# Beacon attention followed by a two-layer feed-forward net: the first batch in an order written out by hand

## The chip, the cores and the metric

The kernel runs on one core of a Trainium2 chip. A core has five engines that run side by side, each through its own list of instructions in order: TensorE (matrix products, PE in the profile), VectorE (DVE), ScalarE (ACT), GpSimd (POOL) and SyncE (SP). They wait for one another by semaphores. Data comes from the chip's main memory by DMA; a DMA is issued by one of the engines, and 16 DMA engines carry it out. The metric is the time of the program on the device in microseconds (us), lower being better.

## The reference

There are 8 batches of 8 heads with 576 positions of 64 elements, and each head has 16 beacon positions ahead of its keys and values, which every query may see. The other keys are seen causally. The attention's output is laid out as 4608 tokens of 512 elements and goes through two layers with a leaky rectifier between them.

```python
k_all = np.concatenate([beacon_k, k], axis=2)
v_all = np.concatenate([beacon_v, v], axis=2)
scores = scale * np.matmul(q, k_all.transpose(0, 1, 3, 2))
causal[:, Nb:] = np.triu(np.ones((S, S), dtype=bool), k=1)
scores = np.where(causal, -1000000000.0, scores)
a = np.exp(scores - scores.max(-1, keepdims=True))
a /= a.sum(-1, keepdims=True) + 1e-09
attn_out = np.matmul(a, v_all)
x = attn_out.transpose(0, 2, 1, 3).reshape(B * S, H * D)
h = x @ w_in                      # 512 -> 2048
g = np.maximum(0.01 * h, h)
out = g @ w_out                   # 2048 -> 512
```

## The kernel before

**Units of work.** Heads are handled in pairs; pair g is number hp = g mod 4 of batch b = g div 4, so there are 32 pairs. Two pairs make a group of four heads, and q and k come per group: `load_qk(b, grp)` issues four DMAs (L139) on GpSimd's queue into the raw buffers `q_raw` and `k_raw`, converted to bfloat16 on the way. `permute` (L149) copies a raw buffer into `q_nat` or `k_nat` with the order of its elements changed. `load_v(b)` (L180 to L190) issues six DMAs of fp32 values on SyncE's queue, and `cast_v` (L198) makes five copies to bfloat16, one for each block of keys, into one of two buffers `v_aug` with a column of ones.

**One pair.** `t_q(g, 0)` and `t_q(g, 1)` transpose q and k on TensorE (L217), and VectorE copies the result out (L222). `score(g, n)`, n from 0 to 3, multiplies (L240) into one of two buffers `sc`, and ScalarE takes the exponential (L251, L255) into `aT`. `masks(g)` multiplies the blocks on the diagonal by a triangle of ones and zeros, in three VectorE instructions (L265, L272, L278). `value(g, 0)` and `value(g, 1)` multiply by V (12 and 18 matmuls, L306; the column of ones gives the sums), and VectorE takes the reciprocal (L315) and scales (L316). The second half reads all five blocks of V. `x_transposes(g)` transposes the result (L328) and copies it into `xT` (L333). Buffers limit how far ahead a pair may run: two sets of `qT` and `kT`, three of `aT`, two of `x_nat`, two of each raw buffer, two of `v_raw`.

**The feed-forward part** is cut into nine chunks of 512 tokens. `moe1` is one of 16 steps of the first layer of a chunk (four matmuls, L342, and a rectifier on ScalarE, L349), `moe2` a quarter of one of its four output tiles in the second (L358, copied out at L367). `fill()` writes down the next such step that is ready; `ready[0]` says how many chunks may be begun. Steps for the first chunk can begin once batch 0's `xT` is complete.

**The order.** Nothing is planned by costs: the program writes each engine's list in the order of its own calls (`tc.manual_schedule`), and an engine never takes a later instruction first. At the head stand the loads: q and k of (0, 0), then of (0, 1); beacon keys on ScalarE's queue; V of batch 0 on SyncE's, held until the first load of k has landed; w_in in four parts and q and k of batch 1 on GpSimd's. After a first `beacon_transposes`, `permute` of (0, 0) in halves and the transposes of pair 0, the main loop runs over g. In round g it writes the transposes of pair g + 1, scores of pair g, values of pair g - 1, and `x_transposes` of pair g - 2, and at the end `masks(g)`. For batch 0 there are some special steps in it:

- in round 0, behind the scores, the beacon transposes for all other batches, `cast_v(0)` on VectorE and the permutes of (0, 1) on VectorE, and only then `masks(0)`;
- in round 1, the four loads of w_out on GpSimd's queue;
- in round 2, `load_v(1)`, held until the second exponential of pair 2 is done, and the permutes of (1, 0) on GpSimd; in round 3 those of (1, 1) and `cast_v(1)` on GpSimd;
- in round 4, the last values and transposes of batch 0, then `ready[0] = 1` and three fills ahead of the transposes of pair 4.

The lines of the head and of round 0 that matter:

```python
        load_v(0, after=first[1])
        make_mask()
        make_ones()
        for i in range(4):
            load_w_in(i)
...
            if g == 0:
                beacon_transposes(1, B)
                cast_v(0, nc.vector)
                for which in range(2):
                    permute(0, 1, which, nc.vector.tensor_copy)
...
            if has(g):
                masks(g)
```

Of the kernel before, what the change touches and what calls it, by code (L numbers as in the profile page):

```python
# [15 lines left out]
def kernel(  # L16
# [50 lines left out]

    singles = ctx.enter_context(tc.tile_pool(name="singles", bufs=1))
    rawpool = ctx.enter_context(tc.tile_pool(name="rawpool", bufs=2))
    natpool = ctx.enter_context(tc.tile_pool(name="natpool", bufs=3))  # L70
    headpool = ctx.enter_context(tc.tile_pool(name="headpool", bufs=2))
    gpool = ctx.enter_context(tc.tile_pool(name="gpool", bufs=2))
# [34 lines left out]
            nc.gpsimd.memset(t[:, :, :, D : D + 1], 1.0)  # L107

    def load_w_in(i):
        nc.gpsimd.dma_start(  # L110
            out=w_in_sb[:, :, i * 512 : (i + 1) * 512], in_=w_in_r[:, :, i * 512 : (i + 1) * 512]
        )

# [9 lines left out]
    def load_qk(b, grp):  # L123


        qk_raw[b, grp] = (
            rawpool.tile([128, 2, RI, D], BF16, name="q_raw"),
            rawpool.tile([128, 2, RI, D], BF16, name="k_raw"),
        )
        nat[b, grp] = (  # L130
            natpool.tile([128, RI, 2, D], BF16, name="q_nat"),
            natpool.tile([128, RI, 2, D], BF16, name="k_nat"),
        )
# [12 lines left out]
    def permute(b, grp, which, copy, p0=0, p1=128):  # L146

        src, dst = qk_raw[b, grp][which], nat[b, grp][which]
        copy(out=dst[p0:p1], in_=src[p0:p1].rearrange("p h i d -> p i h d"))  # L149

# [22 lines left out]

    v_raws = {}

    def load_v(b, after=None):

        t = rawpool.tile([128, NKB, H, D], FP32, name="v_raw")
        v_raws[b] = t
        first = nc.sync.dma_start(out=t[0:NB, 0], in_=beacon_v[b].rearrange("h p d -> p h d"))  # L180
        if after is not None:
            tc.add_manual_dep(
                first.ins,
                after.ins.name,
                mybir.DependencyInfo(mybir.DependencyClass.Sync, mybir.DependencyReason.DATA),
                reason="loads in order of need",
            )
        nc.sync.dma_start(out=t[NB:128, 0], in_=v[b, :, 0:112].rearrange("h p d -> p h d"))
        for c in (1, 2, 3, 4):
            nc.sync.dma_start(  # L190
                out=t[0 : ROWS[c], c],
                in_=v[b, :, OFF[c] : OFF[c] + ROWS[c]].rearrange("h p d -> p h d"),
            )

    def cast_v(b, eng):
        t, dst = v_raws.pop(b), v_bufs[b % 2]
# [205 lines left out]
    with order:  # L402
# [1 line left out]
        make_identity(nc, ident)  # L404
        load_qk(0, 1)
        load_beacon_k()
        load_v(0, after=first[1])
        make_mask()
        make_ones()
        for i in range(4):  # L410
            load_w_in(i)
        load_qk(1, 0)
        load_qk(1, 1)
# [4 lines left out]
            permute(0, 0, 1, nc.scalar.copy, e * RP, (e + 1) * RP)  # L418
        t_q(0, 0)
        t_q(0, 1)  # L420

        def loads(g):
            b, hp = divmod(g, NPAIR)
            if 1 <= b < B - 1:
# [7 lines left out]
            if hp == 3 and b < B - 1:  # L432
                cast_v(b + 1, nc.gpsimd)

        for g in range(NG + 2):
            b, hp = divmod(g, NPAIR)
            if has(g):
                loads(g)
            if g == NPAIR:

                value(g - 1, 0)
                x_transposes(g - 2)
                value(g - 1, 1)
                x_transposes(g - 1)
                ready[0] = 1
                for n in range(3):
                    fill()
                t_q(g, 0)
# [16 lines left out]
                if slots[n]:  # L465
                    fill()

            if has(g + 1) and g + 1 != NPAIR:
                t_q(g + 1, 0)
            if has(g):  # L470
                score(g, 0)
                last = score(g, 1)
                if g == 2:
                    load_v(1, after=last)
            slot(0)
            if has(g - 2) and g - 2 != NPAIR - 1:
# [5 lines left out]
            if has(g - 1):  # L482
                value(g - 1, 0)
            slot(2)
            slot(3)
            if has(g + 1) and g + 1 != NPAIR:
# [5 lines left out]
            if has(g - 1):  # L492
                value(g - 1, 1)
            slot(5)
            slot(6)
            if g == 0:
                beacon_transposes(1, B)
                cast_v(0, nc.vector)
                for which in range(2):
                    permute(0, 1, which, nc.vector.tensor_copy)  # L500
            if g == 1:
                for i in range(4):
                    load_w_out(i)
            if has(g):
                masks(g)
            slot(7)
# [32 lines left out]
```

## Time and profile before

| what | value |
|---|---|
| time, median of 3 runs | 390.72 us (389.57 to 391.29) |
| the profiled execution, time | 390.62 us |
| its span | 388.9 us |
| TensorE busy | 352.4 us, 91% of the span |
| VectorE, ScalarE, GpSimd busy | 176.6, 197.9, 99.5 us |
| first matmul of the feed-forward part (L342) | 53.72 us from the start of the span |
| bytes moved by DMA | 33.52 MB |

The page cuts the span into 40 equal slices of 9.7 us. A digit is the busy share of a slice in tenths.

```profile
PE   2306689999999999999999999999999999999996
DVE  3307956965555655465546554655455331101021
ACT  4304439945575556555655566456645623343310
POOL 8306336876204520462046203200000000000000
DMA  8996999777343913482248225100010001101012
```

From the seventh slice on TensorE is full to the last one. In the first six it isn't, and the third slice has no digit above zero on any compute engine, while the row of the DMA engines is full there.

Times in the prediction are microseconds from the start of the span. In a timeline the first two numbers of a row are the start and the length; a row that ends in "x12" merges twelve instructions, and the length is from the first one's start to the last one's end.

### The profile page before, as it was taken

What the parts mean: (1) busy time and instruction counts of PE and PEld (TensorE: products, weight loads), DVE (VectorE), ACT (ScalarE), POOL (GpSimd) and SP (SyncE); (2) the same over time, 40 slices, a digit from 0 to 9 for tenths busy, and PEclk for the clock granted to TensorE, in tenths of its full rate; (3) what the DMA queues carried; (4) which work ended last, traced back from release to release, by engine and by line L of the source; (5) the groups of instructions that cost most, each with busy time, mean ns of one, the idle gap of its engine ahead of it and who ended that gap; (6) DMA issues with size and microseconds to landing.
All of it is one profiled execution on the core that took longest, in us unless ns stands there. A gap on an engine that the chain in (4) does not pass through costs nothing.

```text
span 388.9 us, 7644 instructions
## 1 busy us (share of the span) xinstructions
PE 352.4 (91%) x3240; PEld 183.7 (47%) x3240; DVE 176.6 (45%) x401; ACT 197.9 (51%) x308; POOL 99.5 (26%) x145
## 2 busy tenths in 40 slices
PE   2306689999999999999999999999999999999996
PEld 1104455655555555555555555555555454444442
DVE  3307956965555655465546554655455331101021
ACT  4304439945575556555655566456645623343310
POOL 8306336876204520462046203200000000000000
PEclk9999689999999999999999999999999999999999
DMA  8996999777343913482248225100010001101012
GB/s 132 202 197 90 186 206 199 142 112 123 71 96 58 161 46 82 71 140 66 76 78 128 77 65 91 56 29 27 2 56 29 28 9 47 55 1 54 29 54 81
DMA packets 58354, 33.52 MB, mean 86 GB/s; under 512 B 41424, under 2 KB 53712, under 8 KB 58320
## 3 DMA queue, kind: packets, MB, share of 16 engines
q0 software_dynamic: 13440, 13.64, 23.2%
q1 hardware_dynamic: 43840, 19.14, 20.3%
q8 instruction: 25, 0.41, 0.4%
q10 hardware_dynamic: 1040, 0.26, 0.3%
q14 instruction: 9, 0.07, 0.1%
HBM read 37.22 MB, written 9.44 MB: 120 GB/s over the span
## 4 chain that ended last, share of the span: by engine, by line
PE 88%; DMA 5%; DVE 2%; SPq 2%; ACT 0%; issue 0%; POOL 0%; DVEq 0%; POOLq 0%
PE acc L358 33%; PE acc L342 33%; PE av L306 8%; PE sc L240 7%; PE tp L217 5%; DMA v_raw<-in_v_dram 4%; PE tp L328 2%; SPq L190 2%; DVE aT L265 1%; DMA k_raw<-in_k_dram 1%; DVE aT L272 0%; ACT aT L251 0%; DVE x_nat L316 0%; DVE q_nat L149 0%; POOL q_raw L139 0%
## 5 line engine op out<-in xcount | busy, mean ns | idle before, releaser
L342 PE MATMUL acc<-xT,w_in_sb 128*128 128x512 bf16 x576 | 145.0, 380 | 0.0
L349 ACT ACTIVATE gT<-acc 128x512 bf16<-128x512 f32 x144 | 85.8, 598 | 110.6 <-PE acc L342 110.5
L358 PE MATMUL acc<-w_out_sb,gT 128*128 128x512 bf16 x576 | 142.0, 380 | 0.0
L251 ACT ACTIVATE aT<-sc 128x928 bf16<-128x928 f32 (+2 forms) x128 | 102.7, 857 | 58.4 <-PE sc L240 58.4
L358 PEld LDWEIGHTS <-gT 128*128 128x128 bf16 x576 | 51.2, 98 | 61.5 <-issue 7.5
L342 PEld LDWEIGHTS <-w_in_sb 128*128 128x128 bf16 x576 | 52.5, 98 | 56.0 <-issue 2.9
L367 DVE COPY osb<-acc 128x512 f32<-128x512 f32 x36 | 24.9, 691 | 58.6 <-PE acc L358 57.2
L306 PEld LDWEIGHTS <-aT 128*128 128x128 bf16 (+1 forms) x960 | 39.2, 101 | 20.1 <-DVE aT L265 4.4
L306 PE MATMUL av<-v_aug,aT 128*128 128x65 bf16 (+1 forms) x960 | 42.6, 198 | 5.4 <-DVE aT L265 4.1
L240 PE MATMUL sc<-qT,kT 64*128 64x208 bf16 (+5 forms) x384 | 43.1, 302 | 1.7 <-DVE kT L222 1.0
L222 DVE COPY qT<-tp 128x576 bf16<-128x576 bf16 x32 | 24.1, 753 | 28.2 <-PE tp L217 28.1
L149 POOL COPY q_nat<-q_raw 128x1152 bf16<-128x1152 bf16 x14 | 16.2, 1155 | 78.8 <-PE tp L217 72.4
L315 DVE RECIPROCAL rec<-av 128x6 f32<-128x6 f32 x64 | 12.0, 188 | 53.3 <-PE av L306 53.2
L217 PE MATMUL tp<-ident,q_nat 64*128 64x64 bf16 x288 | 14.7, 197 | 20.1 <-DVE q_nat L149 20.1
L316 DVE TENSOR_TENSOR x_nat<-av,rec 128x384 bf16<-128x384 f32 x64 | 31.4, 491 | 2.2
L222 DVE COPY kT<-tp 128x576 bf16<-128x576 bf16 x32 | 24.2, 756 | 16.6 <-PE tp L217 16.6
L333 DVE COPY xT<-tp 128x576 bf16<-128x576 bf16 x32 | 14.6, 456 | 27.2 <-PE tp L328 27.1
L198 POOL CAST v_aug<-v_raw 128x512 bf16<-128x512 f32 (+1 forms) x35 | 22.5, 682 | 15.0 <-DMA v_raw<-in_v_dram 12.6
L217 PEld LDWEIGHTS <-q_nat 64*128 64x128 bf16 x288 | 10.9, 98 | 32.4 <-DVE q_nat L149 20.7
L139 POOL DMA_DIRECT2D q_raw<-in_q_dram x32 | 20.2, 631 | 20.1 <-DVE q_nat L149 19.1
L149 POOL COPY k_nat<-k_raw 128x1152 bf16<-128x1152 bf16 x14 | 16.2, 1160 | 30.8 <-PE tp L217 30.7
L240 PEld LDWEIGHTS <-kT 64*128 64x128 bf16 (+1 forms) x384 | 19.8, 100 | 5.2 <-issue 3.0
(30 smaller groups left out, 158.0 us busy)
## 6 DMA issues: line engine op xcount, KB each, us to landing
out_dram<-osb SPq DMA_DIRECT2D x36, 256.0 KB, 2.0
v_raw<-in_v_dram SPq DMA_DIRECT2D x24, 256.0 KB, 5.2
q_raw<-in_q_dram POOLq DMA_DIRECT2D x32, 144.0 KB, 5.1
k_raw<-in_k_dram POOLq DMA_DIRECT2D x32, 144.0 KB, 5.6
w_in_sb<-in_moe_w_in_dram POOLq DMA_DIRECT2D x4, 512.0 KB, 13.4
w_out_sb<-in_moe_w_out_dram POOLq DMA_DIRECT2D x4, 512.0 KB, 11.8
v_raw<-in_v_dram SPq DMA_DIRECT2D x8, 224.0 KB, 4.3
v_raw<-in_v_dram SPq DMA_DIRECT2D x8, 160.0 KB, 5.1
```

The costliest lines, as they stand in the source:

```text
L149: copy(out=dst[p0:p1], in_=src[p0:p1].rearrange("p h i d -> p i h d"))
L198: eng.tensor_copy(out=dst[0 : ROWS[c], c, :, 0:D], in_=t[0 : ROWS[c], c])
L217: nc.tensor.transpose(ps[:, i * RP : (i + 1) * RP], nat[b, grp][which][ps_, i].rearrange("p h d -> p (h d)"), ident[ps_, ps_],)
L222: nc.vector.tensor_copy(out=dst.rearrange("c (p i) -> c p i", i=RI), in_=ps[:, 0:S].rearrange("c (i p) -> c p i", i=RI),)
L240: nc.tensor.matmul(out=sc[0 : ROWS[c], par, col - c0 : col - c0 + w], lhsT=kT[ps_, c * 128 : c * 128 + ROWS[c]], rhs=qT[ps_, q0 : q0 + w], ...
L251: last = nc.scalar.activation(out=aT[:, :, c0 : c0 + w], in_=sc[:, :, 0:w], func=AF.Exp, scale=0.125)
L306: nc.tensor.matmul(out=avv[:, n, 0 : D + 1], lhsT=aT[0 : ROWS[c], par, a0 : a0 + 128], rhs=va[0 : ROWS[c], c, 2 * hp + par, :], start=(c = ...
L316: nc.vector.tensor_tensor(out=x_nat[:, t0:t1].rearrange("p t e d -> p (t e) d"), in0=avv[:, :, 0:D], in1=rec[:, n0:n1, None].to_broadcast( ...
L342: nc.tensor.matmul(out=acc, lhsT=w_in_sb[:, j, fc * 128 : (fc + 1) * 128], rhs=xT[:, j, i * 512 : (i + 1) * 512], start=(j == 0), stop=(j ...
L349: nc.scalar.activation(out=gT[i][:, fc, :], in_=acc, func=AF.Prelu, alpha=0.01)
L358: nc.tensor.matmul(out=acc, lhsT=gT[i][:, fc, t * 128 : (t + 1) * 128], rhs=w_out_sb[:, fc, :], start=(fc == 0), stop=(fc == NF - 1),)
L367: nc.vector.tensor_copy(out=osb, in_=acc)
```

## The change

Batch 0 leaves the main loop and is written out call by call; the loop begins at round 4. Scores run up to two pairs ahead of the values. `cast_v(0)` and the permutes of (0, 1) change places with other VectorE work. `load_w_in(0)` is made to wait for the last DMA of V of batch 0 (`behind`), and all later work on GpSimd's queue stands behind it. The raw buffers of q and k go from two to four, and the buffers `q_nat` and `k_nat` are taken when the permute is written, not with the load. The loads of w_out move behind the permutes of batch 1 on GpSimd's queue, two behind each group. `load_v(1)` is still held by the second exponential of pair 2. From round 4 on the loop's calls are the same as before.

```diff
+    qkpool = ctx.enter_context(tc.tile_pool(name="qkpool", bufs=4))
...
         qk_raw[b, grp] = (
-            rawpool.tile([128, 2, RI, D], BF16, name="q_raw"),
-            rawpool.tile([128, 2, RI, D], BF16, name="k_raw"),
-        )
...
+            qkpool.tile([128, 2, RI, D], BF16, name="q_raw"),
+            qkpool.tile([128, 2, RI, D], BF16, name="k_raw"),
         )
...
+    def behind(ins, other):
+        tc.add_manual_dep(
+            ins.ins,
+            other.ins.name,
+            mybir.DependencyInfo(mybir.DependencyClass.Sync, mybir.DependencyReason.DATA),
+            reason="loads in order of need",
+        )
...
-        load_v(0, after=first[1])
+        v0 = load_v(0, after=first[1])
         make_mask()
         make_ones()
-        for i in range(4):
+        behind(load_w_in(0), v0)
+        for i in range(1, 4):
             load_w_in(i)
         load_qk(1, 0)
         load_qk(1, 1)
...
         t_q(0, 0)
         t_q(0, 1)
+        score(0, 0)
+        score(0, 1)
+        t_q(1, 0)
+        t_q(1, 1)
+        score(0, 2)
+        score(0, 3)
+        beacon_transposes(1, B)
+        score(1, 0)
+        score(1, 1)
+        masks(0)
+        permute(0, 1, 0, nc.vector.tensor_copy)
+        permute(0, 1, 1, nc.vector.tensor_copy)
+        t_q(2, 0)
+        t_q(2, 1)
+        score(1, 2)
+        score(1, 3)
+        score(2, 0)
+        v1 = score(2, 1)
+        masks(1)
+        cast_v(0, nc.vector)
+        value(0, 0)
+        for which in range(2):
+            permute(1, 0, which, nc.gpsimd.tensor_copy)
+        load_w_out(0)
+        load_w_out(1)
+        for which in range(2):
+            permute(1, 1, which, nc.gpsimd.tensor_copy)
+        load_w_out(2)
+        load_w_out(3)
+
+        score(2, 2)
+        load_v(1, after=v1)
+        score(2, 3)
+        t_q(3, 0)
+        t_q(3, 1)
+        value(0, 1)
+        score(3, 0)
+        score(3, 1)
+        masks(2)
+        x_transposes(0)
+        value(1, 0)
+        score(3, 2)
+        value(1, 1)
+        score(3, 3)
+        x_transposes(1)
+        value(2, 0)
+        value(2, 1)
+        masks(3)
+        x_transposes(2)
+        value(3, 0)
+        value(3, 1)
+        x_transposes(3)
+        cast_v(1, nc.gpsimd)
+        ready[0] = 1
...
-        for g in range(NG + 2):
+        for g in range(NPAIR, NG + 2):
```

More of the change, by code (lines that the diff above doesn't have):

```diff
@@ L181, in load_v @@
         if after is not None:
[L182 to L187, printed above, removed]
+            behind(first, after)
         nc.sync.dma_start(out=t[NB:128, 0], in_=v[b, :, 0:112].rearrange("h p d -> p h d"))
         for c in (1, 2, 3, 4):
-            nc.sync.dma_start(
+            last = nc.sync.dma_start(
                 out=t[0 : ROWS[c], c],
@@ L481 @@
             slot(1)
-            if has(g - 1):
+            if has(g - 1) and g - 1 >= NPAIR:
                 value(g - 1, 0)
@@ L485 @@
             slot(3)
-            if has(g + 1) and g + 1 != NPAIR:
+            if has(g + 1):
                 t_q(g + 1, 1)
```

36 lines of the change are left out of this document (12 added, 24 removed).

## The prediction, on record before the changed kernel ran

> **What bounds the kernel now.** I read the stages first, cut at three instants: the first cast of V, the end of the casts, and the first matmul of the feed-forward part (columns: length of the stage, then busy microseconds and instructions of each engine, granted clock, DMA share, GB/s).
>
> ```profile
> 0.00:14.83 14.83, 5.62 (x56) 3.51 (x56) 5.73 (x12) 7.99 (x9) 11.62 (x26) 1.00 0.98 158
> 14.83:31.46 16.63, 0.00 (x0) 0.00 (x0) 2.06 (x5) 0.00 (x0) 0.00 (x0) 1.00 1.10 181
> 31.46:53.72 22.26, 15.47 (x213) 11.44 (x213) 18.83 (x40) 10.35 (x15) 10.54 (x14) 0.78 1.02 164
> 53.72:388.90 335.18, 331.30 (x2974) 168.73 (x2972) 149.99 (x345) 179.60 (x284) 77.30 (x106) 1.00 0.35 73
> ```
>
> The last stage is TensorE's: busy for 331.30 of 335.18 us. Nothing in it can be won by an order of work at the start; it can only begin earlier. The second stage is empty: 16.63 us without one matmul, and the DMA engines full. The third has TensorE busy for 15.47 of 22.26 us and VectorE for 18.83. So the change is worth what it takes out of the first 53.72 us, less what it makes late behind them.
>
> Why the second stage is empty is in the waits of that window and the timelines of VectorE and TensorE (start, length, instruction; in brackets the idle time before it and its releaser):
>
> ```profile
> DVE v_aug L198 <- DMA v_raw<-in_v_dram: 14.6, 4, 6.2
> ```
> ```profile
> 14.83 0.43 DVE L198 CAST v_aug<-v_raw 128x512 bf16<-128x512 f32 x1
> ...
> 31.12 0.43 DVE L198 CAST v_aug<-v_raw 80x512 bf16<-80x512 f32 x1 [0.39 <-DMA v_raw<-in_v_dram]
> 31.46 0.74 DVE L149 COPY q_nat<-q_raw 128x1152 bf16<-128x1152 bf16 x1
> ...
> 37.47 3.92 DVE L265 TENSOR_TENSOR aT<-aT,mask 128x224 bf16<-128x224 bf16 x1
> 41.31 1.49 DVE L272 TENSOR_TENSOR aT<-aT,mask 128x768 bf16<-128x768 bf16 x1
> ...
> 49.95 0.27 DVE L265 TENSOR_TENSOR aT<-aT,mask 128x224 bf16<-128x224 bf16 x1
> 50.14 0.55 DVE L272 TENSOR_TENSOR aT<-aT,mask 128x768 bf16<-128x768 bf16 x1
> ```
> ```profile
> 13.04 0.93 PE L164 MATMUL tp<-ident,bk 128*128 128x128 bf16 x7
> 32.26 0.55 PE L217 MATMUL tp<-ident,q_nat 64*128 64x64 bf16 x7 [18.29 <-DVE q_nat L149]
> ...
> 53.72 3.08 PE L342 MATMUL acc<-xT,w_in_sb 128*128 128x512 bf16 x12
> ...
> 64.46 0.54 PE L306 MATMUL av<-v_aug,aT 128*128 128x65 bf16 x12
> ...
> 66.64 0.73 PE L306 MATMUL av<-v_aug,aT 128*128 128x65 bf16 x18
> ```
>
> VectorE runs in order. Its five casts of V (14.83 to 31.12) wait 14.6 us for V's DMAs, and the copy of q_nat at 31.46, which TensorE's transposes at 32.26 need, is queued behind them. That data had landed long before. V is not needed by the scores at all.
>
> V is late for a reason that the DMA views show. The first answer is the window 6 to 12 us, the second 16 to 28, the third 52 to 58; q0 holds GpSimd's loads, q1 those of SyncE (packets, MB, share of the engines). The fourth is one load of q on an idle queue, issued at 32.50, the fifth the first load of V of batch 1, issued beside w_out (size, time to landing).
>
> ```profile
> q1 hardware_dynamic: 1201, 0.30, 24.8%
> ```
> ```profile
> q0 software_dynamic: 1878, 1.88, 91.8%
> q1 hardware_dynamic: 1874, 0.47, 29.6%
> ```
> ```profile
> q1 hardware_dynamic: 4715, 1.18, 101.0%
> ```
> ```profile
> q_raw<-in_q_dram POOLq DMA_DIRECT2D x1, 144.0 KB, 3.0
> ```
> ```profile
> v_raw<-in_beacon_v_dram SPq DMA_DIRECT2D x1, 32.0 KB, 6.0
> ```
>
> While both queues have work they pass the same number of packets (1878 and 1874 in 12 us), and V's are a quarter as large: q0 gets 0.157 MB/us and V 0.039. Alone V gets 1.18/6 = 0.20. So V crawls until w_in is through.
>
> **The change part by part.** The sizes are in the list of DMA issues (median time to landing last), and the issuing engines' rows say when:
>
> ```profile
> v_raw<-in_v_dram SPq DMA_DIRECT2D x24, 256.0 KB, 5.2
> q_raw<-in_q_dram POOLq DMA_DIRECT2D x32, 144.0 KB, 5.1
> ...
> w_in_sb<-in_moe_w_in_dram POOLq DMA_DIRECT2D x4, 512.0 KB, 13.4
> ...
> v_raw<-in_v_dram SPq DMA_DIRECT2D x8, 224.0 KB, 4.3
> v_raw<-in_v_dram SPq DMA_DIRECT2D x8, 160.0 KB, 5.1
> ...
> v_raw<-in_beacon_v_dram SPq DMA_DIRECT2D x8, 32.0 KB, 3.1
> ```
> ```profile
> 7.50 3.00 POOL L110 DMA_DIRECT2D w_in_sb<-in_moe_w_in_dram  x4
> ...
> 34.90 3.04 POOL L115 DMA_DIRECT2D w_out_sb<-in_moe_w_out_dram  x4
> 37.87 1.21 POOL L149 COPY q_nat<-q_raw 128x1152 bf16<-128x1152 bf16 x1
> ...
> 41.13 1.25 POOL L149 COPY k_nat<-k_raw 128x1152 bf16<-128x1152 bf16 x1
> ...
> 57.47 0.61 POOL L198 CAST v_aug<-v_raw 80x512 bf16<-80x512 f32 x1 [0.20 <-DMA v_raw<-in_v_dram]
> ```
> ```profile
> 6.04 0.38 SPq L180 DMA_DIRECT2D v_raw<-in_beacon_v_dram  x1
> ...
> 39.58 0.33 SPq L180 DMA_DIRECT2D v_raw<-in_beacon_v_dram  x1
> ```
>
> *Weights behind V.* One batch of V is 32 + 224 + 3 x 256 + 160 KB = 1.21 MB. It is issued at 6.04 as now; 0.30 MB had moved by 12 us, and from there w_in no longer competes, so the other 0.91 MB at 0.20 take 4.6 us: V of batch 0 lands at about 16.6 instead of 31. The bounds are 12.1 (alone from its issue) and 18.0 (all of it from 12 on). The added wait stands on GpSimd's queue, and behind it stand the other three loads of w_in, the eight loads of q and k of batch 1, their permutes, w_out and the casts of V of batch 1. All of them start some 9 us later than w_in does now (7.50).
>
> *Four raw buffers for q and k.* The loads of (1, 1) no longer wait for the permute of (0, 1). They follow at once, still behind w_in.
>
> *Casts later on VectorE, scores ahead.* With V in at 16.6, the casts no longer hold VectorE. The new order has them behind the masks of pair 1. What remains of stages two and three is their work: 22.26 us, less the stall of the two mask rows at 37.47 and 41.31 (3.92 + 1.49 against 0.27 + 0.55 of the rows at 49.95 and 50.14: 4.6 us), plus five casts of 0.43 (2.15). From 14.83 that gives 34.6, with nothing waiting. With the mask stall kept it gives 39.2. To choose I walked the new order engine by engine. Besides the rows above it uses these, of ScalarE, TensorE and VectorE:
>
> ```profile
> 10.74 3.10 ACT L251 ACTIVATE aT<-sc 128x1024 bf16<-128x1024 f32 x4 [1.16 <-PE sc L240]
> ```
> ```profile
> 33.66 0.84 PE L306 MATMUL av<-v_aug,aT 128*128 128x65 bf16 x12
> ...
> 35.70 1.17 PE L306 MATMUL av<-v_aug,aT 128*128 128x65 bf16 x18
> ```
> ```profile
> 9.28 0.75 DVE L222 COPY kT<-tp 128x576 bf16<-128x576 bf16 x1
> ```
>
> The walk: the beacon transposes end at 13.97 as now, masks of pair 0 end at 15.7, the two permutes of group 1 at 17.0, the two transposed copies of pair 2 (0.75 each) at 18.5. ScalarE then does the last two exponentials of pair 1 and two of pair 2 at about 0.9 each, so the one that releases V of batch 1 ends at 21.4 (now 39.58). Casts of V end at 22.6, and V has been there for 6 us. From there each pair's values (0.84 + 1.17 on TensorE, with a reciprocal and a multiply behind each half) alternate with masks: masks of pair 2 end at 26.9, values of pair 1 at 29.2, of pair 2 at 32.5, masks of pair 3 at 34.0, values of pair 3 at 35.8, its transposes at 36.9. I take 36.7 for the first feed-forward matmul, near the middle of 34.6 and 39.2. That is 17.0 us ahead of 53.72.
>
> *What is late next.* Three fills stand before the transposes of pair 4. q and k of (1, 0) must be there: GpSimd issues w_in at 16.7. A load takes 3.0 us of which 144 KB at 0.157 are 0.9, so 2.1 are latency. w_in (4 x 512 KB) and four loads of 144 KB are 2.69 MB, or 17.1 us, so they land at 35.9. Two permutes, 1.15 us each by the spacing of the rows from 37.87 to 41.13, end at 38.2, and the transposes come at 36.7 + 3.1 = 39.8 (the row at 53.72 is the three fills). That just holds.
>
> V of batch 1 doesn't hold. It is issued at 21.4 into a queue shared with w_in, then q and k, then w_out. Its latency lies between 2.1 us and the 5.2 of the load beside w_out (6.0, less 0.8 for 32 KB at 0.039); I take 3.6, the middle. From 25.0 it crawls at 0.039 until q0 runs dry, 17.1 + 3.8 us behind the first byte of w_in, at 39.7: 0.57 MB. Behind that w_out waits for the permute of (1, 0), 38.2, and its latency of 2.1. I take a gap of 1 us, worth 0.2 MB. The remaining 0.44 MB crawl beside w_out for 11.3 us, to 52.0. GpSimd's last cast (0.61 in the row at 57.47) ends at 52.6. The second value half of pair 4 needs that cast. Now it runs at 66.64, 12.9 us behind the first feed-forward matmul, and ends at 67.37; behind 36.7 it would end at 50.3. With the cast at 52.6 and half of its 18 matmuls left it ends at 53.0. The gain is 67.37 - 53.0 = **14.4 us**, of the 17.0 that batch 0 gives. With no gap q0 would be through with w_out at 53.1 and V right behind it, so the cast would end at 54.5 at the latest; with a gap of 3 us it is early enough not to matter. The chunks of w_out, moved behind the permutes, are covered by the first layer's 16 fills: 64 matmuls at 3.08/12 us alone reach from 36.7 to 53.1, attention stands between them, and the first chunk is in by then; without that cover each us of its lateness would be one of the end. Everything behind the values of pair 4 is the present stage, moved. It keeps its length.
>
> The profiled execution took 390.62 us, 1.72 more than its span of 388.9, and the median of the runs is 390.72. So the forecast is 390.62 - 14.4 = **376.2 us**.
>
> **The rivals.** *V of batch 1 comes in time.* If q0's gap is longer or the release is earlier, only batch 0's end counts: 390.62 - 17.0 = 373.6. Against it stands the equal packet count of the two queues; for it, that 0.6 MB or more has landed before w_out starts.
>
> *GpSimd's permutes stop the masks again.* The masks at 37.47 and 41.31 took 4.6 us too long exactly while four permutes ran on GpSimd (37.87 to 42.38), and the same masks at 49.95 did not. In the new order the permutes come whenever q and k of batch 1 land. I have that at 35.9, two microseconds behind the masks of pair 3 (34.0). If they land sooner or the masks run later, the first feed-forward matmul goes to 41.3, the value half ends at 55.0 and the gain is 12.4: 378.2. The Trainium skill has this as a rule ("SBUF — State Buffer", Who interferes with whom): VectorE and GpSimd share a pair of ports, and a VectorE instruction with two SBUF inputs is blocked by a GpSimd instruction that reads SBUF for as long as that one runs. By that rule, the trace agrees (3.92 us against 0.27).
>
> *V of batch 0 isn't faster.* If V lands at 31 as now even without w_in beside it, w_in starts there too. q and k of (1, 0) then land at 50.3, the permutes end at 52.6, and the transposes of pair 4 follow there instead of at 53.72 + 3.1 = 56.8: 386.4. The 0.20 MB/us of the window 52 to 58 speaks against it.
>
> *GpSimd's loads become the bound, slower than before.* They start 9 us later, and VectorE is now at work while they are issued and drained. If that halved q0 to 0.07 MB/us, q and k of (1, 0) would land at 57.2, the transposes of pair 4 at 59.5 instead of 56.8: 393.3. It decides below 0.071. Against it: four loads of w_out at 34.90, beside a busy VectorE, were issued in 3.04 us, and four of w_in at 7.50 in 3.00.
>
> **How the numbers follow.** Forecast 0.50 (374.5 to 378), V in time 0.22, masks stopped 0.20, V no faster 0.05, loads the bound 0.03. The range goes from 371.5 (first feed-forward matmul at 34.6, V in time) to 381.0 (batch 0 at its slow bound of 39.2 and the masks stopped for another 4.6 us). About 0.5% or 2 us is what a measurement of this kernel can tell from no change; only the last rival is slower by that: faster 0.95, same 0.02, slower 0.03.
>
> **What would show it.** Right: no hole in TensorE between 14 and 31; the last cast of V of batch 0 on VectorE at 22 to 23, with no DMA wait before it; w_in issued at 16 to 18; first feed-forward matmul at 36 to 38; the last cast of V of batch 1 at 51 to 55 and a wait of 1 to 4 us before the second value half of pair 4. The steps fail if that wait is missing (V in time), if a mask of pair 2 or 3 takes over 1 us (masks stopped), or if the transposes of pair 4 wait for GpSimd's copies. The sum would be wrong most of all if the feed-forward part, once it starts, took longer than its 335.18 us.

## The result, and the profile after

The changed kernel takes 378.78 us (median of 4 runs, 377.94 to 380.7) against 390.6 us (median of the kernel before in the same round, 4 runs): a ratio of 0.9706, 95% interval 0.9664 to 0.9749. Measured again later, on one chip with two of the other kernels, it was 378.89 us (median of 5 runs), ratio 0.9688 (0.9667 to 0.9709). A run over 1.5% above the fastest of its kernel counts as slow and is left out of the ratios; that is one run, of 380.05 us, of the ninth experiment. The forecast was 376.2 us with a range of 371.5 to 381.0. The profiled execution took 380.7 us, with a span of 379.0; it is the longest of the four, so what is read from it is up to 2 us more than the median has.

The span, cut at the first feed-forward matmul, at the last matmuls of the second value half of pair 4, at the transposes of pair 8, and behind each of the last two at the end of a stretch of lower clock (columns as before; the lines of the changed program are six higher, so L348 and L364 are the two feed-forward layers, L312 the values, L223 the transposes of q and k):

```profile
0.00:33.23 33.23, 20.45 (x269) 13.87 (x269) 21.63 (x56) 18.48 (x24) 15.27 (x29) 1.00 1.00 159
33.23:50.66 17.43, 13.25 (x137) 6.76 (x139) 7.27 (x15) 11.41 (x19) 11.32 (x15) 1.00 1.22 205
50.66:54.00 3.34, 3.33 (x23) 1.33 (x22) 1.97 (x6) 0.69 (x2) 3.34 (x6) 0.51 1.21 198
54.00:60.24 6.24, 3.96 (x61) 2.41 (x60) 3.66 (x11) 4.55 (x7) 2.51 (x5) 1.00 1.22 212
60.24:64.30 4.06, 3.83 (x36) 2.06 (x38) 2.51 (x5) 1.86 (x2) 2.56 (x3) 0.58 0.95 177
64.30:379.00 314.70, 307.08 (x2668) 157.38 (x2717) 137.64 (x309) 161.28 (x255) 65.96 (x91) 1.00 0.32 70
```

The empty stage is gone: TensorE is busy for 20.45 of the first 33.23 us. Later on there are two short stretches in which TensorE's granted clock is 0.51 and 0.58 on the mean, most of the time 0.50. The timeline of TensorE shows what stands ahead of each:

```profile
20.64 1.05 PE L312 MATMUL av<-v_aug,aT 128*128 128x65 bf16 x12 [0.30 <-DVE v_aug L204]
...
33.23 2.81 PE L348 MATMUL acc<-xT,w_in_sb 128*128 128x512 bf16 x11
37.56 0.43 PE L223 MATMUL tp<-ident,q_nat 64*128 64x64 bf16 x9 [1.52 <-POOL q_nat L151]
38.65 0.43 PE L223 MATMUL tp<-ident,k_nat 64*128 64x64 bf16 x9 [0.66 <-POOL k_nat L151]
39.02 1.90 PE L348 MATMUL acc<-xT,w_in_sb 128*128 128x512 bf16 x8
...
50.66 0.49 PE L312 MATMUL av<-v_aug,aT 80*128 80x65 bf16 x6 [1.83 <-POOL v_aug L204]
50.96 1.90 PE L348 MATMUL acc<-xT,w_in_sb 128*128 128x512 bf16 x4
...
60.24 0.38 PE L223 MATMUL tp<-ident,q_nat 64*128 64x64 bf16 x7 [2.23 <-POOL q_nat L151]
```

V of batch 0 is in in time: TensorE waits 0.30 us for its cast (20.64). The first feed-forward matmul comes at 33.23 instead of 53.72, **20.5 us** sooner. Then come three new waits: 1.52 and 0.66 us at the transposes of pair 4, for GpSimd's permutes of q and k of (1, 0); 1.83 us in the second value half of pair 4, for the last cast of V of batch 1; and 2.23 us at the transposes of pair 8, for the permute of q of (2, 0). GpSimd's timeline has the other side of them:

```profile
17.68 4.55 POOL L111 DMA_DIRECT2D w_in_sb<-in_moe_w_in_dram  x4 [9.87 <-DMA v_raw<-in_v_dram]
...
26.92 0.59 POOL L136 DMA_DIRECT2D k_raw<-in_k_dram  x1 [1.70 <-DMA w_in_sb<-in_moe_w_in_dram]
30.24 0.59 POOL L136 DMA_DIRECT2D q_raw<-in_q_dram  x1 [2.73 <-DMA w_in_sb<-in_moe_w_in_dram]
33.62 0.59 POOL L136 DMA_DIRECT2D k_raw<-in_k_dram  x1 [2.79 <-DMA w_in_sb<-in_moe_w_in_dram]
36.37 1.14 POOL L151 COPY q_nat<-q_raw 128x1152 bf16<-128x1152 bf16 x1 [2.16 <-DMA q_raw<-in_q_dram]
...
50.00 0.61 POOL L204 CAST v_aug<-v_raw 80x512 bf16<-80x512 f32 x1 [3.33 <-DMA v_raw<-in_v_dram]
...
56.47 0.59 POOL L136 DMA_DIRECT2D k_raw<-in_k_dram  x1 [1.75 <-DMA w_out_sb<-in_moe_w_out_dram]
59.05 1.14 POOL L151 COPY q_nat<-q_raw 128x1152 bf16<-128x1152 bf16 x1 [1.98 <-DMA q_raw<-in_q_dram]
```

w_in is issued at 17.68, released by V; the permutes at 36.37 and 59.05 and the cast at 50.00 each begin when a DMA lands. To see where the 20.5 us went, set the same instructions of both kernels side by side. In the kernel before they were here:

```profile
57.36 1.90 PE L342 MATMUL acc<-xT,w_in_sb 128*128 128x512 bf16 x8
...
67.21 1.03 PE L342 MATMUL acc<-xT,w_in_sb 128*128 128x512 bf16 x4
...
72.80 0.37 PE L217 MATMUL tp<-ident,q_nat 64*128 64x64 bf16 x7
```

| instruction | before | after | gain |
|---|---|---|---|
| first feed-forward matmul | 53.72 | 33.23 | 20.5 |
| first feed-forward matmul behind the transposes of pair 4 | 57.36 | 39.02 | 18.3 |
| the one behind the values of pair 4 | 67.21 | 50.96 | 16.2 |
| transposes of pair 8 | 72.80 | 60.24 | 12.6 |
| end of the span | 388.9 | 379.0 | 9.9 |

Half of what batch 0 won is given back, 10.6 us: about 2 us at each of the first two waits, 3.6 us from the value half to the transposes of pair 8 (2.23 of it a wait), and 2.7 us behind them. A last wait, of 0.95 us, is in these 2.7:

```profile
79.95 0.38 PE L348 MATMUL acc<-xT,w_in_sb 128*128 128x512 bf16 x1 [0.95 <-DVE xT L339]
```

What is not a wait is the clock. At 39.02 eight feed-forward matmuls take 1.90 us. At 50.96, behind the wait and in the stretch with a clock of 0.51, four take as long. As an estimate from the rows of the two stretches, 3.34 us at 0.51 and 4.06 us at 0.58 lose 1.6 and 1.7 us. With the waits (1.52, 0.66, 1.83, 2.23 and 0.95, together 7.2) that is 10.5 of the 10.6 us.

### The profile page after: what moved, and what is told of

Its sections match the earlier page's. It is cut to its first block, busy times and chain, and to the rows that moved or that the text cites. A ratio compares the mean times of both kernels' runs of the same rounds, so it can differ in the third digit from the quotient of the medians.

```text
span 379.0 us, 7607 instructions
## 1 busy us (share of the span) xinstructions
PE 351.9 (93%) x3186; PEld 183.8 (48%) x3240; DVE 174.7 (46%) x401; ACT 198.3 (52%) x308; POOL 101.0 (27%) x145
## 4 chain that ended last, share of the span: by engine, by line
PE 81%; DMA 8%; POOL 4%; issue 2%; DVE 2%; SPq 2%; POOLq 0%
PE acc L364 33%; PE acc L348 30%; PE av L312 6%; PE sc L246 5%; DMA q_raw<-in_q_dram 5%; PE tp L223 4%; PE tp L334 2%; SPq L195 1%; POOL w_in_sb L111 1%; DMA v_raw<-in_v_dram 1%; DMA k_raw<-in_k_dram 1%; POOL v_aug L204 1%; POOL k_nat L151 1%; POOL q_nat L151 1%; POOL q_raw L136 1%
## 5 line engine op out<-in xcount | busy, mean ns | idle before, releaser
L348 PE MATMUL acc<-xT,w_in_sb 128*128 128x512 bf16 x548 | 144.6, 382 | 2.7 <-DVE xT L339 0.9
L364 PE MATMUL acc<-w_out_sb,gT 128*128 128x512 bf16 x550 | 139.8, 380 | 1.4 <-issue 0.2
L364 PEld LDWEIGHTS <-gT 128*128 128x128 bf16 x576 | 51.2, 98 | 61.5 <-issue 7.5
L348 PEld LDWEIGHTS <-w_in_sb 128*128 128x128 bf16 x576 | 52.6, 98 | 56.5 <-issue 3.7
L312 PEld LDWEIGHTS <-aT 128*128 128x128 bf16 (+1 forms) x960 | 38.7, 100 | 17.3 <-issue 3.2
L246 PE MATMUL sc<-qT,kT 64*128 64x208 bf16 (+5 forms) x384 | 43.8, 307 | 2.8 <-DVE kT L228 1.7
L312 PE MATMUL av<-v_aug,aT 128*128 128x65 bf16 (+1 forms) x960 | 41.8, 197 | 2.4 <-POOL v_aug L204 1.8
L151 POOL COPY k_nat<-k_raw 128x1152 bf16<-128x1152 bf16 x14 | 16.2, 1154 | 29.7 <-PE tp L223 29.6
L136 POOL DMA_DIRECT2D k_raw<-in_k_dram x32 | 20.3, 633 | 6.2 <-DMA w_in_sb<-in_moe_w_in_dram 4.5
L278 DVE TENSOR_TENSOR aT<-aT,mask 128x768 bf16<-128x768 bf16 x32 | 20.7, 647 | 1.0 <-ACT aT L257 1.0
L223 PE MATMUL tp<-ident,q_nat 64*128 64x64 bf16 x288 | 15.0, 198 | 6.6 <-POOL q_nat L151 3.8
```

What stands on the lines that cost most here:

```text
L223: nc.tensor.transpose(ps[:, i * RP : (i + 1) * RP], nat[b, grp][which][ps_, i].rearrange("p h d -> p (h d)"), ident[ps_, ps_],)
L246: nc.tensor.matmul(out=sc[0 : ROWS[c], par, col - c0 : col - c0 + w], lhsT=kT[ps_, c * 128 : c * 128 + ROWS[c]], rhs=qT[ps_, q0 : q0 + w], ...
L312: nc.tensor.matmul(out=avv[:, n, 0 : D + 1], lhsT=aT[0 : ROWS[c], par, a0 : a0 + 128], rhs=va[0 : ROWS[c], c, 2 * hp + par, :], start=(c = ...
L348: nc.tensor.matmul(out=acc, lhsT=w_in_sb[:, j, fc * 128 : (fc + 1) * 128], rhs=xT[:, j, i * 512 : (i + 1) * 512], start=(j == 0), stop=(j ...
L364: nc.tensor.matmul(out=acc, lhsT=gT[i][:, fc, t * 128 : (t + 1) * 128], rhs=w_out_sb[:, fc, :], start=(fc == 0), stop=(fc == NF - 1),)
```

## The experiments

The theory after this reading: the change brings batch 0 forward by 20 us, and the loads of the first 60 us, which were not in the way before, now are. Each wait for one of them can bring a stretch at half clock behind it. The rivals: the hold of w_in brings little and the order of scores and values brings the gain, or the other way round; the second and third wait come from where the loads stand on GpSimd's queue and not from the bytes ahead of them. Each edit is to the changed kernel unless it says otherwise.

**V of batch 1 without its hold**

```diff
         v0 = load_v(0, after=first[1])
+        load_v(1)
...
-        v1 = score(2, 1)
+        score(2, 1)
...
-        load_v(1, after=v1)
```

> V of batch 1 is issued right behind V of batch 0, not behind the second exponential of pair 2; nothing else changes. Theory (loads are late, and each wait brings a stretch at half clock): V of batch 1 moves at full rate in the hole between V of batch 0 and w_in (17 to 19 us, about 0.4 MB) and is in before 44, so the wait of 1.8 us ahead of the second value half of pair 4 goes, with the half clock behind it, and GpSimd gets to the loads of q and k of batch 2 at 47.3 instead of 50.6, so that the wait at the transposes of pair 8 shrinks too: 373 to 375 us against 378.8. Rival (the loss behind 51 us is not from these waits, or V then takes from w_in what it gains): the wait at the transposes of pair 4 grows and the time is within 1 us of 378.8.

Measured: 381.52 us, ratio 0.976 (0.9728 to 0.9793), slower than the changed kernel. The theory missed, and so did the time of the rival (within 1 us of 378.8), though the wait that it named did grow. The wait for V of batch 1 went, but the one at the transposes of pair 4 grew to 4.34 us (timeline of TensorE):

```profile
40.91 0.58 PE L223 MATMUL tp<-ident,q_nat 64*128 64x64 bf16 x9 [4.34 <-POOL q_nat L151]
...
62.89 0.38 PE L223 MATMUL tp<-ident,q_nat 64*128 64x64 bf16 x7 [2.42 <-POOL q_nat L151]
```

V of batch 1 went ahead of w_in, and V of batch 2, now next on SyncE's queue, ran beside w_in and q and k of (1, 0). Those landed 3.3 us later than in the changed kernel (permutes from 39.71 instead of 36.37). So a load moved forward pushes back another. That V takes nothing from GpSimd's queue, as the prediction had it, began to look wrong.

**q and k of batch 2 ahead of the casts**

```diff
+        load_qk(2, 0)
         cast_v(1, nc.gpsimd)
         ready[0] = 1
...
-                if hp < 2:
+                if hp < 2 and (b + 1, hp) not in qk_raw:
                     load_qk(b + 1, hp)
```

> The loads of q and k of the first group of batch 2 stand ahead of the casts of V of batch 1 on GpSimd's queue. Theory (the wait at the transposes of pair 8 comes from the order on GpSimd's queue: these loads stand behind a cast that waits for V): that wait of 2.2 us goes and the half clock behind it, the wait before the values of pair 4 stays or grows by up to 2 us, since the casts come 2.4 us later: 375 to 378 us. Rival (these loads are late because the DMA engines are full, wherever they stand): the wait stays, and with later casts the time is 379 to 381.

Measured: 379.6 us, ratio 0.9693 (0.9645 to 0.9741). The loads are issued 6.8 us sooner and land at the same time: the wait stays, and is 3.71 us instead of 2.23 (timelines of GpSimd and TensorE):

```profile
43.76 0.62 POOL L136 DMA_DIRECT2D q_raw<-in_q_dram  x1
...
58.87 1.14 POOL L151 COPY q_nat<-q_raw 128x1152 bf16<-128x1152 bf16 x1 [2.07 <-DMA q_raw<-in_q_dram]
```
```profile
60.07 0.55 PE L223 MATMUL tp<-ident,q_nat 64*128 64x64 bf16 x7 [3.71 <-POOL q_nat L151]
```

The rival holds: they are late because of the bytes ahead of them (w_out, with V beside it), not because of their place behind a cast.

**w_in not held**

```diff
-        behind(load_w_in(0), v0)
-        for i in range(1, 4):
+        for i in range(4):
             load_w_in(i)
```

> w_in is not made to wait for V of batch 0; all else is as changed. Theory (the hold is worth what batch 0 gains from an early V, less the waits that it makes later): V of batch 0 lands at about 31 as in the kernel before, its casts hold up only the values, and the first feed-forward matmul comes at 31.5 + 11.3 = 43 instead of 33.2; but q and k of batch 1, V of batch 1 and q and k of batch 2 are in time, so nothing is given back later: 379 to 381 us, about the same as with the hold. Rival (the hold is what the change is worth): V late costs its full 10 us: 387 to 390.

Measured: 384.97 us, ratio 0.9856 (0.9824 to 0.9888), between the two forecasts. The waits of TensorE from 13 to 66 us (total, times, longest):

```profile
PE av L312 <- DVE v_aug L204: 10.5, 4, 4.4
```

V of batch 0 arrives in pieces, and TensorE waits 10.5 us for its casts; the first feed-forward matmul was expected at 43 and came at 47.23, since the last block of V was cast only at 34.2. But hardly anything is given back behind it: from there to the end it is 336.1 us, against 335.2 in the kernel before; in all four runs the granted clock is 1.0, and they lie within 0.25%. The hold is worth 6 us of the whole. Without it the rest of the change still brings the first feed-forward matmul forward by 6.5 us (53.72 to 47.23) and the time down by 5.5 us: on VectorE, masks and copies that don't need V now stand ahead of the casts.

**The hold alone, in the kernel before** (`load_v` and `load_w_in` return their last instruction for it)

```diff
-        for i in range(4):
+        w0 = load_w_in(0)
+        tc.add_manual_dep(w0.ins, v0.ins.name, ...)
+        for i in range(1, 4):
             load_w_in(i)
```

> The kernel before, with the hold of w_in behind V of batch 0 alone: no order by hand, no more raw buffers. Theory: the casts of V on VectorE end at about 18, and the rest of batch 0 takes the 17.7 us that it took before without the stalled masks, so the first feed-forward matmul comes at 35 to 37; but w_out now stands ahead of the permutes of batch 1 on GpSimd's queue and of V of batch 1 in the DMA engines, so the transposes of pair 4 wait until 45 or so: 381 to 385 us. Rival (the order by hand is what the change is worth, the hold alone brings nothing): 388 to 391.

Measured: 383.17 us, ratio 0.9808 (0.9763 to 0.9853). The first feed-forward matmul comes at 33.99, 0.8 us behind the changed kernel's, although scores and values stand in the loop's old order:

```profile
33.99 2.82 PE L343 MATMUL acc<-xT,w_in_sb 128*128 128x512 bf16 x11
```
```profile
38.38 0.43 PE L218 MATMUL tp<-ident,q_nat 64*128 64x64 bf16 x9 [1.58 <-POOL q_nat L149]
...
52.00 0.38 PE L307 MATMUL av<-v_aug,aT 128*128 128x65 bf16 x4 [3.53 <-POOL v_aug L199]
```

So the hold by itself makes batch 0 as short. The loads behind it are worse: the values of pair 4 wait 3.53 us for V of batch 1. The long wait that was expected at the transposes of pair 4 (until 45) did not come; they stand at 38.38.

**The hold, and w_out behind the permutes, in the kernel before** (the hold as above)

```diff
                 for which in range(2):
                     permute(b + 1, hp - 2, which, nc.gpsimd.tensor_copy)
+                if b == 0:
+                    load_w_out(2 * hp - 4)
+                    load_w_out(2 * hp - 3)
...
-            if g == 1:
-                for i in range(4):
-                    load_w_out(i)
```

> The hold of w_in in the kernel before, as in e4_hold_alone, and the loads of w_out moved behind the permutes of batch 1, two behind each group; the scores and values of batch 0 stay in the loop's order. Theory (what the change has beyond the hold is the order of the loads alone, not that scores run ahead): the permutes of (1, 0) and V of batch 1 come earlier, and the time falls from 383.2 to that of the changed kernel, 378 to 380 us. Rival (the order of scores and values by hand brings those 4 us): it stays at 382 to 384.

Measured: 379.92 us, ratio 0.973 (0.9674 to 0.9787), which can't be told from the changed kernel's 0.9688. The hold and the place of w_out bring what the whole change brings; with the hold in place, the order by hand of scores, casts and values has no gain that these runs show.

**V of batch 2 held**

```diff
                 score(g, 2)
-                score(g, 3)
+                load_v(2, after=score(g, 3))
...
-                if hp == 0:
+                if hp == 0 and b > 1:
                     load_v(b + 1)
```

> The changed kernel, with V of batch 2 held until the last full exponential of pair 4. Theory (all queues share one rate of 0.20 MB/us, so what V of batch 2 moves is taken from the loads that are waited for): the hold takes V of batch 2 out of the stretch in which V of batch 1 is already waited for only if it comes late enough; the exponential ends at about 45 and V of batch 1 is on the queue until 50, so little changes before 50 and the wait at the transposes of pair 8 shrinks by at most 1 us: 378 to 379.5. Rival (V of batch 2 has nothing to do with it): the same time and the same wait of 2.2 us.

Measured: 378.97 us, ratio 0.9689 (0.9653 to 0.9724): no difference from the changed kernel, and the wait at the transposes of pair 8 is 3.18 us, where at most 2.2 was expected by either account. With both theories near 379 the run decides little; the hold ended at 47.9, too soon to keep V of batch 2 out of the way.

**w_in released by the third block of V**

```diff
-            last = nc.sync.dma_start(
+            ins = nc.sync.dma_start(
...
-        return last
+            if c == 2:
+                third = ins
+        return third
```

> The changed kernel, with w_in held by the third block of V of batch 0 (c = 2) instead of the last. Theory (one shared byte rate, so the hole of 2 to 3 us between the end of V and the first bytes of w_in is lost to all later loads): w_in is issued at about 15, its bytes begin when V ends, V is still in before its casts at 20, and q and k of (1, 0) land at 34 instead of 36: the wait at the transposes of pair 4 shrinks from 2.2 to under 0.5 us, the later ones too: 376 to 378. Rival (the last blocks of V crawl beside w_in): the last cast of V waits until 24 or later, batch 0 ends later by as much, 380 or more.

Measured: 377.29 us, ratio 0.9641 (0.9606 to 0.9676). w_in is issued at 16.17, q and k of (1, 0) land two microseconds sooner, and the wait at the transposes of pair 4 is gone. The other two were expected to shrink and did not (1.84 and 3.40 us):

```profile
16.17 3.00 POOL L111 DMA_DIRECT2D w_in_sb<-in_moe_w_in_dram  x4 [8.36 <-DMA v_raw<-in_v_dram]
...
34.25 1.14 POOL L151 COPY q_nat<-q_raw 128x1152 bf16<-128x1152 bf16 x1 [1.99 <-DMA q_raw<-in_q_dram]
```
```profile
48.58 0.35 PE L314 MATMUL av<-v_aug,aT 80*128 80x65 bf16 x6 [1.84 <-POOL v_aug L206]
...
57.82 0.47 PE L225 MATMUL tp<-ident,q_nat 64*128 64x64 bf16 x7 [3.40 <-POOL q_nat L151]
```

**V of batch 1 without its hold, V of batch 2 held**: the edits of the first and the sixth experiment together.

> V of batch 1 right behind V of batch 0, as in e1_v1_no_hold, and V of batch 2 held until the last full exponential of pair 4. Theory (one shared byte rate): V of batch 1 is in at 22, nothing runs beside w_in and q and k of batch 1, which then move at 0.20 instead of 0.157 MB/us; q and k of (1, 0) land at 33 to 34 instead of 39.6, so the wait of 4.3 us at the transposes of pair 4 goes; w_out is through at 47 and q and k of (2, 0) land by 52: no wait above 0.5 us and no half clock, 371 to 374 us. Rival (GpSimd's queue moves 0.157 MB/us whatever runs beside it, as the prediction had it): q and k of (1, 0) land at 38.5, and the time is 379 to 381.

Measured: 377.0 us, ratio 0.9652 (0.9604 to 0.9699). The DMA view of the window 28 to 36 us, first of the changed kernel, then of this one (packets, MB, share of the engines):

```profile
q0 software_dynamic: 1236, 1.24, 90.8%
q1 hardware_dynamic: 1237, 0.31, 29.2%
```
```profile
q0 software_dynamic: 1600, 1.61, 121.4%
q1 hardware_dynamic: 49, 0.01, 1.1%
```

This settles the rate. With V beside them, GpSimd's loads move 1.24 MB in 8 us, 0.155 MB/us, and V 0.039. Without V they move 1.61, 0.20 MB/us. The sum is the same to some 4%: what V moves is taken from the others. The wait at the transposes of pair 4 fell from 4.34 us in the first experiment to 1.05. But the time is between the 371 to 374 us of the theory and the 379 to 381 of the rival, and the permute of q of (1, 0) began at 36.62, where the theory had that data in by 34. The waits did not all go either: q and k of (2, 0) were again waited for, 3.37 us; w_out stood ahead of them, and V of batch 2, released at 45.8, ran beside them.

**The loads in order of need**

```diff
         v0 = load_v(0, after=first[1])
+        load_v(1)
...
+        load_w_out(0)
         for which in range(2):
             permute(1, 0, which, nc.gpsimd.tensor_copy)
-        load_w_out(0)
+        load_qk(2, 0)
         load_w_out(1)
         for which in range(2):
             permute(1, 1, which, nc.gpsimd.tensor_copy)
-        load_w_out(2)
-        load_w_out(3)
...
         cast_v(1, nc.gpsimd)
+        load_qk(2, 1)
+        load_w_out(2)
+        load_w_out(3)
```

with w_in released by the third block of V, and V of batch 2 held, as above; the loop's own calls for the loads that are moved are left out.

> The loads in the order in which they are needed, on top of e7_w_in_sooner: V of batch 1 right behind V of batch 0; on GpSimd's queue one part of w_out ahead of the permutes of (1, 0), then q and k of (2, 0) and the second part of w_out, the permutes of (1, 1), the casts of V of batch 1, q and k of (2, 1), the rest of w_out; V of batch 2 held until the last full exponential of pair 4. Theory (after the change the first 60 us are bound by the order of bytes at 0.20 MB/us, so nothing but that order separates it from the 20 us that batch 0 won): no wait above 0.5 us at the transposes of pair 4, at the values of pair 4 or at the transposes of pair 8, no half clock after 35 us, and 371 to 374 us, under e7's 377.3. Rival (the waits are a matter of total bytes, and move from one load to another): a wait of 2 us or more appears at V of batch 2 or at w_out, and the time is 376 to 378.

Measured: 375.64 us (6 runs, 373.45 to 380.05), ratio 0.9603 (0.9569 to 0.9637), against 0.9688 (0.9667 to 0.9709) for the changed kernel on the same chip: faster than that one, but over the 371 to 374 us that was expected. It can't be told apart from the seventh and eighth experiments, whose intervals overlap with its own. The profiled execution took 373.45 us and is the fastest of the six. Its stages, cut at the first feed-forward matmul and at the transposes of k of pair 8 (those of q come at 55.21, without a wait):

```profile
0.00:33.70 33.70, 20.75 (x268) 13.97 (x269) 21.64 (x56) 18.52 (x24) 15.33 (x30) 1.00 1.12 182
33.70:58.00 24.30, 21.74 (x258) 11.49 (x258) 16.33 (x33) 18.70 (x30) 21.68 (x28) 1.00 1.21 203
58.00:371.70 313.70, 309.85 (x2717) 157.43 (x2716) 135.37 (x313) 161.01 (x255) 64.66 (x89) 1.00 0.33 72
```
```profile
37.45 0.43 PE L225 MATMUL tp<-ident,q_nat 64*128 64x64 bf16 x9 [0.91 <-POOL q_nat L151]
38.54 0.43 PE L225 MATMUL tp<-ident,k_nat 64*128 64x64 bf16 x9 [0.66 <-POOL k_nat L151]
```

The clock is 1.00 in every stage of this execution; in the other five its mean is 0.989 to 0.995, so they had stretches of lower clock. Of the three waits only the first is left (0.91 and 0.66 us, not under the 0.5 of the theory), and no new one came at V of batch 2 or at w_out, against the rival. From the transposes of q of pair 8 to the end it is 316.5 us (55.21 to 371.7), as in the kernel before (316.1) and against 318.8 in the changed kernel. So the moves together were worth another 3 us over the changed kernel, with the same bytes and with batch 0 no shorter (33.73 instead of 33.23 to the first feed-forward matmul).

**Two raw buffers instead of four**

```diff
-    qkpool = ctx.enter_context(tc.tile_pool(name="qkpool", bufs=4))
+    qkpool = ctx.enter_context(tc.tile_pool(name="qkpool", bufs=2))
```

> The changed kernel with two raw buffers for q and k instead of four. Theory (the buffers are free by 17 us, before the loads that need them are issued at 22): no load moves and the time is that of the changed kernel, 378 to 380 us. Rival (the loads of batch 1 or 2 wait for a buffer): the transposes of pair 4 or pair 8 wait longer, 381 or more.

Measured: 379.67 us, ratio 0.9706 (0.9685 to 0.9727). The buffers bring nothing that can be measured.

**The changed kernel again**

> The changed kernel itself, for a comparison on the same chip as e9_by_need and e10_two_raw: 378 to 380 us, with the three waits seen before (transposes of pair 4, second value half of pair 4, transposes of pair 8).

Measured: 378.89 us, as above. Its profiled execution (381.14 us, the longest of five) has three stretches at half clock instead of two, at 32.6, 39.4 and 59.9 us; the first two last 3.4 us each and the third 6.8. The mean granted clock is 0.982:

```profile
core 0: 379.4 us, clock 0.982
```

Only two of the three expected waits are there, at the transposes of pair 4 (0.95 and 0.66 us) and of pair 8 (3.91). The one for V of batch 1 is not: TensorE, slowed down from 32.6 on, came later to those values.

## Why the prediction held, and where it didn't

*The bound and its cause: right.* V was late because it shared the DMA engines with w_in, and VectorE's casts held up work that didn't need V. With the hold w_in goes out at 17.68 (forecast 16.7), and the casts wait for nothing. The experiment with the hold alone shows that this is the cause: it makes the 20 us in batch 0 by itself. The experiment without the hold shows the other half: with the casts moved and V as late as before, batch 0 is 6.5 us shorter.

*The walk through batch 0: a term too large.* It gave 36.7 for the first feed-forward matmul; 33.23 was measured, even below the bound of 34.6 that was called free of waits. The size that failed most is that of the values on TensorE, taken as 0.84 + 1.17 us a pair from rows at 33.66 and 35.70 of the kernel before. In the changed kernel that holds only until about 26 us, as the values of pairs 0, 1 and 2 show in the timeline of TensorE:

```profile
23.36 1.17 PE L312 MATMUL av<-v_aug,aT 128*128 128x65 bf16 x18
...
27.03 0.73 PE L312 MATMUL av<-v_aug,aT 128*128 128x65 bf16 x18
...
28.62 1.08 PE L312 MATMUL av<-v_aug,aT 128*128 128x65 bf16 x30
```

18 matmuls fall from 1.17 to 0.73 us, and all 30 of pair 2 take 1.08 where the walk had 2.01. Over pairs 1 to 3 this is some 2.1 of the 3.5 us; another 0.7 was won before, as the casts ended at 21.9 and not 22.6. The rows of the walk came from just behind the empty stage. The granted clock reads 1.00 there and through the first 33 us of the changed kernel, so it doesn't tell the two sizes apart, and why the same matmuls get shorter is not shown. The bound of 34.6 had another fault: it was cut out of a stage whose row in the prediction has a clock of 0.78, and in the changed kernel that stage runs at 1.00.

*q and k of (1, 0): the size right, the verdict wrong.* They were forecast to land at 35.9, and the permute began at 36.37. "That just holds" fell because TensorE was there 3.5 us sooner. A wait of the transposes of pair 4 for GpSimd's copies was named as a sign that the steps fail, and it came (1.52 and 0.66 us).

*V of batch 1: right.* Forecast: last cast at 52.6 and a wait of 1 to 4 us. Measured: 50.61 and 1.83 us. The value half ended 16.2 us sooner where 14.4 was forecast, since TensorE and V both came sooner.

*"Everything behind the values of pair 4 is the present stage, moved. It keeps its length": this step failed.* From the matmul behind those values to the end it was 388.9 - 67.21 = 321.7 us before and is 379.0 - 50.96 = 328.0 now: 6.3 us more in the profiled executions, and 1.9 us less than that by the median, as 380.7 is that much above it. The prediction had named the sign itself: the feed-forward part, once it starts, takes 345.8 us (33.23 to 379.0) and not 335.18. The stage had been bound by TensorE because its loads had slack. Moved forward by 16 us it used up that slack: q and k of (2, 0) came 2.23 us late, and TensorE ran at half clock for a while behind this wait and behind the one for V of batch 1. The prediction followed the loads up to V of batch 1 and stopped there. Behind this stands its rate: it gave GpSimd's queue 0.157 MB/us whatever ran beside it. The eighth experiment shows 0.20 for both queues together, so it should have added up the bytes that must land before the transposes of pair 8.

The two errors have opposite signs, and so the time came out only 2.6 us above the forecast. That it came so close is in part luck: 378.78 lies outside the 374.5 to 378 that the forecast had its chance of 0.50 for, and is nearest to the 378.2 of stopped masks, which in batch 0 did not happen. (The upper end of the range is also 0.3 us above what its own terms give, 390.62 - (53.72 - 43.8) = 380.7.)

*The rivals.* The masks of batch 0 were not stopped: those of pair 3 stand at 30.44 and take 0.27 and 0.55 us, well before GpSimd's permutes at 36.37. They were stopped later, beside four permutes that begin at 75.04, as the timeline of VectorE shows:

```profile
75.25 1.06 DVE L271 TENSOR_TENSOR aT<-aT,mask 128x224 bf16<-128x224 bf16 x1
76.23 1.49 DVE L278 TENSOR_TENSOR aT<-aT,mask 128x768 bf16<-128x768 bf16 x1
77.65 1.22 DVE L284 TENSOR_TENSOR aT<-aT,mask 80x256 bf16<-80x256 bf16 x1
```

Together they take 3.8 us instead of 1.1. The copy into `xT` stands behind them, and for that copy the matmul at 79.95 waited its 0.95 us. This agrees with the rule of the Trainium skill that the prediction cites; but in the kernel before a mask was held for 3.92 us, the time of three permutes of 1.2 us and not of one. V was faster, and GpSimd's loads did not become slower than before. V of batch 1 was not in time. The prediction gave the move of w_out a hidden cost and no gain. In the experiments it is the only part of the change that may bring something beyond the hold, some 3 us (383.17 to 379.92); the intervals of the two, 0.9763 to 0.9853 and 0.9674 to 0.9787, overlap, so this is not shown.

What stays open: why some waits are followed by a stretch at half clock and others of the same length are not (1.83 us in the changed kernel was, 1.84 us in the seventh experiment was not), why the changed kernel, run again, had such a stretch at 32.6 with no wait over 0.33 us in the 5 us ahead of it, and which of the moves in the ninth experiment did most.

## What to carry to other kernels

When a stall at the start goes, all that follows comes sooner, its loads' deadlines too. So list the loads in the order in which the shortened kernel needs them, add up their bytes at the rate that all queues share, and compare with the time at which each is wanted. A hold that puts one load ahead of another is worth what the first user gains less what the held loads lose. With the loads in a better order, the order by hand of the compute engines brought nothing more here; without the hold of w_in it was part of what won 5.5 us.

## What the runs showed of the hardware

- Two queues with work take turns packet by packet (1236 and 1237 packets in 8 us), so that the queue with small packets gets little: 0.31 MB of 256-byte rows against 1.24 MB. The sum, counted at the destination, stays near 0.20 MB/us.
- GpSimd's queue can stop at the issue of a DMA. In the changed kernel the sixth load of q and k of batch 1 stood 1.70 us, and the next two 2.73 and 2.79 us, until a part of w_in had landed (rows at 26.92, 30.24 and 33.62); the same came at 56.47 behind w_out. All else on that queue waits with it. The permute behind it still waited 2.16 us for its data, so these stops do not show up as a loss of their own here.
- Part of the spread from run to run goes with the granted clock. With a mean of 1.0 (w_in not held) four runs lay within 0.25%; the changed kernel had 6.8 us at half clock in one profiled execution and 13.7 in another. It is not all: two runs of the changed kernel at 0.990 and 0.991 took 380.7 and 378.88 us.
- The stretches at half clock last about 3.4 us or twice that: 3.4 us at 50.5 and at 60.7 in the changed kernel, and 3.4, 3.4 and 6.8 us when it was run again.
